# A fused attention and mixture-of-experts kernel: a new order of the attention's steps, a third transposed q/k buffer, and sums of x spread over expert 1

## The chip, the core and the metric

The kernel runs on one core of a Trainium2 chip. A core has a tensor engine for matmuls (PE, with its weight loads shown apart as PEld), a vector engine (DVE), a scalar engine (ACT), a general engine (POOL) and a queue engine (SP), each with its own queue of instructions that it works off in order. Matmuls write to eight banks of PSUM; everything else lies in SBUF. Transfers are issued from a queue (SP or POOL, here also ACT at the start) and run on 16 shared DMA engines. The metric is the device time of one execution in microseconds.

## The reference, cut to what matters

```python
# attention: batch 8, heads 8, seq 576, head_dim 64, 128 features
def phi(x):
    proj = np.einsum('bhsd,df->bhsf', x, w_phi)
    proj = proj - np.max(np.abs(proj), axis=-1, keepdims=True)
    return np.concatenate([np.exp(proj), np.exp(-proj)], axis=-1)
q_p, k_p = (phi(q), phi(k))
kv = np.einsum('bhsf,bhsd->bhfd', k_p, v)
z = np.sum(k_p, axis=2)
num = np.einsum('bhsf,bhfd->bhsd', q_p, kv)
den = np.einsum('bhsf,bhf->bhs', q_p, z)[..., None] + 1e-06
attn = num / den
# experts: N = 4608 tokens, D = 512, E = 8, F = 1024; x is attn, heads side by side
logits = x @ w_gate
P = np.exp(logits - logits.max())
for _ in range(8):
    P /= P.sum(1, keepdims=True) + 1e-09
    P /= P.sum(0, keepdims=True) + 1e-09
    P *= N / E
for e in range(E):
    h = np.maximum(x @ w1[e], 0.0)
    out += P[:, e:e + 1] * (h @ w2[e])
```

Every expert works on every token; P only weighs its result.

## The kernel before, in words

**A plan, then four fixed queues.** The program first writes down operations, each with its engine, an estimated duration, and the keys that it reads and writes (`Plan.op`). Then `Plan.schedule` plays them: again and again it takes the operation that can start earliest by the estimates, and among equals the one written down first. `Clock` stands for the tensor clock, `Links` for the two transfer lines (one for SP's and ACT's transfers, one for POOL's). What comes out is a fixed order of instructions for each engine; on the chip each engine follows it and waits where data isn't there. So the order in which steps are written down, and every estimate, change the order on all queues, while the instructions stay.

**Buffers.** A `Ring` is a fixed number of slots of one shape; an operation that needs a slot waits until the slot's last user is done. The ones that matter: `qk` (2, half a batch of k and q in bf16), `v_m` (2, half a batch of v), `qkT` (2, k and q transposed, 4 KB per partition each), `qk_r` and `v_r` (2 each, the last 64 tokens of up to three batches), `hT` (4), and later `S` (5) and `X` (3).

**Attention** goes by pairs of heads, 32 in all, four to a batch, 512 of 576 tokens each; the last 64 tokens of every batch are "rests". The steps are letters. `a` (pair_a) multiplies a pair's transposed k with w_phi (L568), takes maxima on DVE (L560), exponentials on ACT (L564), and v times a factor on POOL (L756). `q` does the q scores and their maxima, `p` the transposed q features. `b` (pair_b) makes the k-v products, `n` and `m` the two heads' outputs (L851, L859 to L865), `c` (pair_c) transposes them into xT, which is on the tensor engine for batches 0, 1, 2 and 7 and by a DMA from SP for 3, 4, 5 and 6 (L874). `r` and `g` are the rests' counterparts of `a` and `c`; `g` also makes the routing logits. `u` and `d` are quarters of a group's up and down products of expert 0, plain matmuls of 512 columns, 24 and 20 of which stand among the attention's steps.

k and q of batches 0 and 1 are loaded as fp32 into buffers that are still empty and transposed on the tensor engine (L698). Those of batches 2 to 7 are loaded by POOL in half batches and converted to bf16 on the way (L496), and turned by a DMA transpose on SP (`turn_qk`, L513, 512 KB). In the kernel before, a load and its turn are issued inside step `a` of the batch ahead: at pairs 0 and 2 of batch b the halves 0 and 1 of batch b+1, each after the maxima of q of the pair before (the key `("max", 0, i - 1)`). Expert 0's weights come in eight slices at pairs 2 to 9, from POOL: four of W1 by columns (L472), four of W2 by rows (L477). An up unit reads the W1 slice of its own columns.

**After the attention** its buffers are given back ("late"), the eight rounds of routing run on DVE with a small matmul each (L1104 to L1115), and what is left of expert 0 runs on the tensor engine. Experts 1 to 7 run over nine groups of 512 tokens with seven products in place of eight for a 2 by 2 blocking (`up7`, `down7`, all matmuls at L1250). That needs four differences of blocks of x per group, `sums_x` (L1158, S<-xT): they are written to DRAM (`xd`, L1234) and read back for every expert (L1240, X<-xd). Before, all nine groups' sums are written down ahead of expert 1, each in two slots of S; `down7` uses four slots of S per group for its own differences of hT.

The lines that carry the steps of the change:

```python
gt = [("max", 0, i - 1)] if i >= 1 else []        # stage_a: the load's gate
ring(a_t, [128, 2, 8, 128], BF16, "qkT", 2)
if e == 1:
    for g in range(NG):
        sums_x(g)
```

Of the kernel before, what the change touches and what calls it, by code (L numbers as in the profile page):

```python
# [108 lines left out]
class Op:  # L109
    __slots__ = ("eng", "dur", "lat", "nbytes", "fn", "left", "ready", "users", "idx", "end",  # L110
                 "bufs", "deps", "shared", "turn", "tiled")

    def after(self, user):

        if user.eng == self.eng and not self.nbytes:
            return self.end - self.lat + (0.0 if self.eng == "PE" else 0.04)
        return self.end


class Links:  # L120
# [6 lines left out]
    def add(self, o, at):  # L127
        n = int(o.eng == "POOL")
        self.line[n].append([at + (2.6 if n else 1.65), o.nbytes / 1e3, o])
# [4 lines left out]
    def step(self, t, work):  # L134
# [5 lines left out]
        if len(on) == 2:  # L140
            share = [0.23, 0.59] if self.line[0][0][2].turn else [0.59, 0.42]
# [48 lines left out]
class Plan:  # L190
# [9 lines left out]
    def op(self, eng, dur, lat, fn, r=(), w=(), takes=(), nbytes=0, shared=False):  # L200
# [5 lines left out]
        o.shared, o.turn, o.tiled = shared, False, 0  # L206
# [42 lines left out]
    def schedule(self):  # L249
# [22 lines left out]
        while len(done) < len(self.ops) or links.next():  # L272
# [28 lines left out]
            else:  # L301
                o.end = at + dur + o.lat
# [11 lines left out]
def kernel(  # L314
# [74 lines left out]
    SPEED = {320: 322, 150: 171, 230: 400, 250: 311, 280: 415, 90: 226, 148: 216, 160: 300}  # L389

    def dma(queue, nbytes, rate, fn, r=(), w=()):

        o = plan.op(queue, 0.8 if queue == "POOL" else 0.6, 0.0, fn, r, w, (),
                    nbytes / SPEED.get(rate, rate))
        o.turn = rate == 148
# [25 lines left out]
    ring(a_in, [128, 3 * NP, 2, D], BF16, "qk_r", 2)  # L421
    ring(a_in, [128, 3 * NP, D], FP32, "v_r", 2)
    ring(a_t, [128, NP, 128], BF16, "rT", 2)
    ring(a_t, [128, 2, 8, 128], BF16, "qkT", 2)
# [42 lines left out]
    def load_w0(i, r):  # L467
# [3 lines left out]
        if i < 4:  # L471
            dma("POOL", 1 << 19, 250, lambda: nc.gpsimd.dma_start(  # L472
                out=w1()[:, :, n * 256:(n + 1) * 256],
                in_=moe_w1[0].rearrange("(c p) f -> p c f", p=128)
                [:, :, n * 256:(n + 1) * 256]), r, [(w1, n)])
# [442 lines left out]
    def up(w1, g, hT, fcs, n, r=(), w=()):  # L918

        for f0 in fcs[::n]:  # L920
            ph = new(f"P{n}")
            ht = hT[f0 // 4]
            for i in range(n):
                for dc in range(NP):
# [3 lines left out]
                        xkeys(g, dc) + [(w1, (f0 + i) // 2), *r], [ph, *w], [ht])  # L928
# [80 lines left out]
    def stage_a(i):  # L1009
        b, pr = i // 4, i % 4  # L1010
        st[i], ms[i], qs[i] = pair_a(b, pr, halves[b, pr // 2])
        gt = [("max", 0, i - 1)] if i >= 1 else []
        if b + 1 < B and pr in (0, 2):
            if b + 1 > 1:
                halves[b + 1, pr // 2] = new_half(b + 1, pr // 2)
            t = halves[b + 1, pr // 2]
            load_qk(b + 1, 2 * pr, 4, t, gt)
            load_v(b + 1, 2 * pr, 4, t, gt)
            if b + 1 >= 2:
                turn_qk(t)  # L1020
        if pr == 1 and b in (0, 1, 4):
            load_rests(b + 1, 1 if b == 0 else 3, gt)
        n = i - 2
        if 0 <= n < 8:
# [483 lines left out]
```

The softmax here doesn't subtract the row's maximum and nothing guards it: scores larger than these inputs give would overflow.

## Time and profile before

| | us |
|---|---|
| median of 6 executions | 1040.15 (1037.38 to 1043.19) |
| the profiled execution's own time | 1041.22 |
| its span, first to last instruction | 1039.4 |
| PE busy, of the span | 1016.6 (98%) |
| PEld | 840.2 (81%) |
| DVE | 821.2 (79%) |
| ACT | 706.3 (68%) |
| POOL | 459.4 (44%) |
| mean granted tensor clock | 0.998 |

How to read it: a matmul's record lasts longer than its place in the pipeline (273 ns for 256 columns, where the next one starts 109 ns later), so a PE that is 98% busy may still lose time; the distance between starts tells. The chain that ended last is followed back from the end, at each step to what released it. A row of the windows has the stretch, its length, then busy time and number of instructions of PE, PEld, DVE, ACT and POOL, the granted clock, the mean busy share of the DMA engines (over 1 where transfers overlap on an engine) and GB/s. SPq is SP's queue; the number after the start is how long the issuing took. In the waits, the three numbers are us in total, times, and the longest.

Stages of the profiled execution: attention with parts of expert 0 to about 213 us, routing and the rest of expert 0 to 263.3, experts 1 to 7 to the end.

### The profile page before, as it was taken

The page shows a single profiled execution, that of the slowest core. Times are in us where ns is not written, and L with a number is a line of the kernel's source. Part 1 is how long each engine was busy: PE and PEld are TensorE (multiplying, and loading weights), DVE is VectorE, ACT ScalarE, POOL GpSimd, SP SyncE. Part 2 cuts the span into 40 slices and gives each one's busy share as a digit, 9 for nine tenths or more (in the row PEclk, how much of TensorE's full clock was granted, in tenths as well). Part 3 has the DMA queues.
Part 4 walks back from the last instruction along what each step waited for, and adds up shares of the span by engine and source line. Part 5 has one row for each costly group of instructions (what it writes and reads, how often), then busy time and mean ns, then how long its engine had stood idle before and what let it go on. Part 6 is the DMA issues. An engine that isn't in the chain of part 4 may idle for free.

```text
span 1039.4 us, 24345 instructions
## 1 busy us (share of the span) xinstructions
PE 1016.6 (98%) x9512; PEld 840.2 (81%) x9512; DVE 821.2 (79%) x1576; ACT 706.3 (68%) x1530; POOL 459.4 (44%) x476
## 2 busy tenths in 40 slices
PE   7889999999999999999999999999999999999998
PEld 5556666644888888888888888888888888888886
DVE  8979998788777787778777887788778877787775
ACT  7979999833788866566666665666666656666663
POOL 5867675400244444434443444344444443334442
PEclk9999999999999999999999999999999999999999
DMA  9999987274511161114311341134111611114333
GB/s 245 160 166 182 178 157 138 43 182 132 103 42 47 47 122 47 48 42 85 80 41 52 82 93 42 42 68 95 42 51 43 132 42 42 42 42 123 133 123 122
DMA packets 113939, 96.02 MB, mean 92 GB/s; under 512 B 54048, under 2 KB 88992, under 8 KB 113824
## 3 DMA queue, kind: packets, MB, share of 16 engines
q1 hardware_dynamic: 80544, 70.55, 27.1%
q0 software_dynamic: 33120, 23.86, 17.2%
q8 instruction: 74, 1.21, 0.5%
q14 instruction: 41, 0.34, 0.1%
q10 hardware_dynamic: 160, 0.07, 0.0%
HBM read 94.98 MB, written 14.16 MB: 105 GB/s over the span
## 4 chain that ended last, share of the span: by engine, by line
PE 89%; DMA 6%; ACT 2%; DVE 1%; POOL 1%; issue 1%; SPq 0%; DVEq 0%; POOLq 0%; ACTq 0%
PE ps L1250 74%; PE ps L568 14%; DMA qkT<-qk 4%; PE ps L851 1%; DMA xd<-S 1%; ACT k L564 0%; DMA acc<-in_q_dram 0%; DMA xT<-xb 0%; ACT q L564 0%; ACT kr L564 0%; POOL vrd L678 0%; PE ps L698 0%; SPq L546 0%; ACT qr L564 0%; POOL qk L496 0%
## 5 line engine op out<-in xcount | busy, mean ns | idle before, releaser
L1405 POOL TENSOR_TENSOR acc<-acc,V 128x512 f32<-128x512 f32 x248 | 316.3, 1285 | 435.3 <-ACT V L1402 418.0
L1278 ACT COPY U<-ps 128x512 f32<-128x512 f32 x378 | 217.3, 587 | 171.9 <-PE ps L1250 162.7
L1282 DVE CUSTOM_DVE_ANT_0 hT<-ps,U 128x512 bf16<-128x512 f32 x378 | 254.3, 686 | 82.8 <-PE ps L1250 57.9
L1402 ACT ACTIVATE V<-ps,P 128x256 f32<-128x256 f32 x496 | 208.7, 474 | 85.6 <-PE ps L1250 78.0
L1390 DVE SCALAR_TENSOR_TENSOR acc<-ps,P,acc 128x256 f32<-128x256 f32 x372 | 159.6, 477 | 78.9 <-PE ps L1250 78.7
L1250 PEld LDWEIGHTS <-S 128*128 128x128 bf16 x1984 | 194.1, 98 | 22.7 <-issue 0.2
L1250 PEld LDWEIGHTS <-T 128*128 128x128 bf16 x1512 | 147.9, 98 | 17.1
L1250 PEld LDWEIGHTS <-hT 128*128 128x128 bf16 x1488 | 145.6, 98 | 16.8
L1250 PE MATMUL ps<-X,T 128*128 128x256 bf16 x1008 | 151.2, 273 | 0.0
L1250 PE MATMUL ps<-T,S 128*128 128x256 bf16 x1056 | 135.8, 273 | 0.1
L1250 PEld LDWEIGHTS <-wx 128*128 128x128 bf16 x1152 | 112.7, 98 | 13.6 <-issue 0.2
L1158 DVE TENSOR_TENSOR S<-hT 128x1024 bf16<-128x1024 bf16 x124 | 87.7, 721 | 9.8 <-ACT hT L1287 9.8
L1250 PEld LDWEIGHTS <-w 128*128 128x128 bf16 x864 | 84.5, 98 | 9.8
L1250 PE MATMUL ps<-xT,wx 128*128 128x256 bf16 x576 | 88.7, 273 | 0.0
L1250 PE MATMUL ps<-X,wx 128*128 128x256 bf16 x576 | 86.5, 273 | 0.0
L1287 ACT ACTIVATE hT<-ps 128x512 bf16<-128x512 f32 x126 | 72.6, 606 | 7.7 <-PE ps L1250 7.7
L1250 PE MATMUL ps<-wx,hT 128*128 128x256 bf16 x560 | 77.6, 273 | 0.0
L1250 PE MATMUL ps<-xT,T 128*128 128x256 bf16 x504 | 76.4, 273 | 0.0
L568 PE MATMUL ps<-xT,w 128*128 128x512 bf16 x288 | 74.7, 379 | 0.0
L568 PE MATMUL ps<-w,hT 128*128 128x512 bf16 x288 | 73.0, 379 | 0.0
L1250 PE MATMUL ps<-T,hT 128*128 128x256 bf16 x496 | 68.4, 273 | 0.0
L1250 PE MATMUL ps<-xT,w 128*128 128x256 bf16 x432 | 67.3, 273 | 0.0
(127 smaller groups left out, 1420.1 us busy)
## 6 DMA issues: line engine op xcount, KB each, us to landing
X<-xd SPq DMA_DIRECT2D x126, 256.0 KB, 2.6
wx<-in_moe_w_dram POOLq DMA_DIRECT2D x8, 1024.0 KB, 10.2
v_m<-in_v_dram SPq DMA_DIRECT2D x15, 512.0 KB, 6.0
out_dram<-acc SPq DMA_DIRECT2D x14, 512.0 KB, 3.1
w<-in_moe_w_dram POOLq DMA_DIRECT2D x6, 1024.0 KB, 9.6
xd<-S SPq DMA_DIRECT2D x18, 256.0 KB, 4.5
qk<-in_k_dram POOLq DMA_DIRECT2D x12, 256.0 KB, 6.1
qk<-in_q_dram POOLq DMA_DIRECT2D x12, 256.0 KB, 7.1
```

The costliest lines, as they stand in the source:

```text
L568: nc.tensor.matmul(out_, lhsT=lhsT, rhs=rhs, start=start, stop=stop)
L851: pe(65, lambda j=j: nc.tensor.matmul(pn()[:, j * D1:j * D1 + D1], lhsT=s["T"][x]()[:, j % 2, 2 * h + j // 2, :] if j < 4 else r["T"][x]() ...
L1158: lambda: f.tensor_tensor(out=out_(), in0=x(), in1=y(), op=op), r, w, **kw)
L1250: pe(256, lambda i=i, k=k, z=z: nc.tensor.matmul(bank()[:, 256 * i:256 * i + 256], lhsT=lhs(k, i), rhs=rhs(k), start=first and z, stop=k = ...
L1278: act(512, lambda: nc.scalar.copy(out=u[fp][n]().rearrange("p a b -> p (a b)"), in_=x[fp]()), [x[fp]], [u[fp][n]])
L1282: dve(515, lambda: nc.vector._custom_dve(ADD_SAT, out=out_(fp, i, j), in0=bank[fp]().rearrange("p (a b) -> p a b", a=2), in1=u[fp][n](), s ...
L1287: act(512, lambda: nc.scalar.activation(out=out_(fp, i, j), in_=x[fp]().rearrange("p (a b) -> p a b", a=2), func=ACT.Relu, bias=0.0, scale ...
L1390: dve(320, lambda n=n, ts=ts: nc.vector.scalar_tensor_tensor(out=acc[g][:, ts, 256 * j:256 * j + 256], in0=bank()[:, 256 * n:256 * n + 256 ...
L1402: act(370, lambda n=n: nc.scalar.activation(out=u()[:, n, :], in_=bank()[:, 256 * n:256 * n + 256], func=ACT.Copy, bias=0.0, scale=P[:, 4 ...
L1405: pool(695, lambda: nc.gpsimd.tensor_tensor(out=acc[g][:, 2 * i:2 * i + 2, 256 * j:256 * j + 256], in0=acc[g][:, 2 * i:2 * i + 2, 256 * j: ...
```

## The change

- The ring `qkT` has 3 slots; `qk_r` and `v_r` hold two batches per slot, not three.
- Loads (`l`), turns (`t`), rests' loads (`e`) and weight slices (`w`) are letters of the order of their own. A load waits for the newest maxima of q and of k written down before it.
- The order is another string. Parts of it that the prediction speaks of: the first load of batch 2 stands behind pair 2, its second behind pair 4; the first two turns behind pairs 5 and 7; two W1 slices behind pair 2, one behind each of pairs 4 and 5; the four of W2 behind pair 8; the first `u` behind the `c` of pair 4. Rests are loaded for 1, 1, 2, 2 and 2 batches.
- W1 of expert 0 is cut by the contracted rows; an up unit needs all four slices.
- `sums_x` is written down for groups 0 and 1 ahead of expert 1, and for group g+2 between group g's up and down products of expert 1, after one of the blocks of hT.
- The planner's estimates change: end of an operation on its own engine, time to the first byte (1.45 and 2.5 us), rates of transfers, and shares of two lines in use together.

```diff
-        self.line[n].append([at + (2.6 if n else 1.65), o.nbytes / 1e3, o])
+        self.line[n].append([at + (2.5 if n else 1.45), o.nbytes / 1e3, o])
...
-            share = [0.23, 0.59] if self.line[0][0][2].turn else [0.59, 0.42]
+            a, b = (x[0][2] for x in self.line)
+            all_ = (0.6 if a.turn else 0.88) / (a.unit + b.unit)
+            share = [all_ * a.unit, all_ * b.unit]
...
-    SPEED = {320: 322, 150: 171, 230: 400, 250: 311, 280: 415, 90: 226, 148: 216, 160: 300}
+    LINK = {320: (312, 55), 150: (168, 28), 230: (410, 66), 250: (300, 50), 280: (410, 54),
+            270: (400, 90), 90: (270, 37), 148: (215, 23), 160: (470, 40)}
...
-    ring(a_in, [128, 3 * NP, 2, D], BF16, "qk_r", 2)
-    ring(a_in, [128, 3 * NP, D], FP32, "v_r", 2)
+    ring(a_in, [128, 2 * NP, 2, D], BF16, "qk_r", 2)
+    ring(a_in, [128, 2 * NP, D], FP32, "v_r", 2)
     ring(a_t, [128, NP, 128], BF16, "rT", 2)
-    ring(a_t, [128, 2, 8, 128], BF16, "qkT", 2)
+    ring(a_t, [128, 2, 8, 128], BF16, "qkT", 3)
...
-            dma("POOL", 1 << 19, 250, lambda: nc.gpsimd.dma_start(
-                out=w1()[:, :, n * 256:(n + 1) * 256],
-                in_=moe_w1[0].rearrange("(c p) f -> p c f", p=128)
-                [:, :, n * 256:(n + 1) * 256]), r, [(w1, n)])
+            dma("POOL", 1 << 19, 270, lambda: nc.gpsimd.dma_start(
+                out=w1()[:, n, :], in_=moe_w1[0].rearrange("(c p) f -> p c f", p=128)[:, n, :]),
+                r, [(w1, n)])
...
-                        xkeys(g, dc) + [(w1, (f0 + i) // 2), *r], [ph, *w], [ht])
+                        xkeys(g, dc) + [(w1, dc), *r], [ph, *w], [ht])
...
-        gt = [("max", 0, i - 1)] if i >= 1 else []
-        if b + 1 < B and pr in (0, 2):
-            if b + 1 > 1:
-                halves[b + 1, pr // 2] = new_half(b + 1, pr // 2)
-            t = halves[b + 1, pr // 2]
-            load_qk(b + 1, 2 * pr, 4, t, gt)
-            load_v(b + 1, 2 * pr, 4, t, gt)
-            if b + 1 >= 2:
-                turn_qk(t)
-        if pr == 1 and b in (0, 1, 4):
-            load_rests(b + 1, 1 if b == 0 else 3, gt)
-        n = i - 2
-        if 0 <= n < 8:
-            load_w0(n, gt)
+
+    def gates():
+
+        seen = order[:at[0]]
+        return [("max", x, seen.count(n) - 1) for x, n in ((0, "q"), (1, "a")) if n in seen]
+
+    def stage_l(n):
+        b, i = 1 + n // 2, n % 2
+        if b > 1:
+            halves[b, i] = new_half(b, i)
+        load_qk(b, 4 * i, 4, halves[b, i], gates())
+        load_v(b, 4 * i, 4, halves[b, i], gates())
+
+    def stage_e(n):
+        load_rests(*((1, 1), (2, 2), (4, 2), (6, 2))[n], gates())
...
-        "arqparqbabqbapqnbaqamqmbnpabqpnpbmnpccnrcnpamqcaqpmbupaqumcacrnbqnuanbqampun"
...
+        "lalareapqbwwlqanalqwaptrwaebbqpnmcpaqtpbmcpmnaqbqwwnmwncrmpcbmqqbwclutpnuapm"
...
     for i, n in enumerate(order):
+        at[0] = i
         STEPS[n](order[:i].count(n))
...
-    def sums_x(g):
+    def sums_x(g, r0=()):
...
-                xkeys(g) + ["late"] + [(X[i // 2], i % 2) for i in r]
+                xkeys(g) + ["late", *r0] + [(X[i // 2], i % 2) for i in r]
...
         if e == 1:
-            for g in range(NG):
+            for g in range(2):
                 sums_x(g)
...
             un = up7(A7, g, X, hT, ["up0"])
+            if e == 1 and g + 2 < NG:
+                later = (g + 2, [(hT[1], 0, 1)])
...
             if dn is not None:
                 dn["out"]()
+            if e == 1 and g + 2 < NG:
+                sums_x(*later)
```

## The prediction

> **What bounds the kernel now.** I read four views of the one profiled execution: the chain that ended last, the stages in windows, the tensor engine's timeline, the SP queue's timeline.
>
> The chain comes first, in order of time. Its second number is a length.
>
> ```profile
> 37.46 16.81 DMA qkT<-qk
> 54.31 1.96 PE ps L568 x9
> 56.27 16.54 DMA qkT<-qk
> ...
> 215.05 7.80 DMA xd<-S
> ...
> 263.34 158.07 PE ps L1250 x1445
> 421.45 606.58 PE ps L1250 x5555
> 1028.04 6.92 PE ps L568 x32
> ```
>
> From 263.34 on the chain is tensor work without a break: 7000 matmuls of 256 columns in 764.7 us, 109.2 ns each, and back to back this shape takes 109. So 776 us (263.3 to 1039.4) are fixed as long as the matmuls stay: the change removes none. What can move is the time at which expert 1 starts, 263.3. Ahead of it the chain names two places: the transposes by DMA (qkT) at 37 to 73, and the writes of the x sums (xd) at 215.
>
> Then the windows: PE busy, weight loads, DVE, ACT, POOL, granted clock, DMA share, GB/s.
>
> ```profile
> 30.00:40.00 10.00, 8.11 (x106) 5.21 (x105) 10.00 (x27) 10.00 (x25) 9.89 (x18) 1.00 1.61 199
> 40.00:50.00 10.00, 8.65 (x119) 6.27 (x120) 9.63 (x25) 9.18 (x23) 6.86 (x11) 1.00 1.45 97
> 50.00:60.00 10.00, 7.12 (x61) 4.22 (x58) 5.46 (x13) 6.44 (x16) 4.88 (x8) 0.83 1.39 179
> 60.00:70.00 10.00, 9.11 (x97) 5.17 (x95) 8.42 (x23) 8.89 (x24) 5.46 (x11) 1.00 1.51 129
> 70.00:80.00 10.00, 8.52 (x114) 5.72 (x112) 9.06 (x21) 9.24 (x25) 8.44 (x12) 1.00 1.26 184
> 80.00:90.00 10.00, 9.89 (x111) 6.72 (x108) 9.31 (x23) 9.29 (x23) 6.91 (x12) 1.00 1.07 187
> ...
> 220.00:230.00 10.00, 7.97 (x39) 3.55 (x38) 7.54 (x22) 3.07 (x6) 0.00 (x0) 1.00 1.13 272
> ```
>
> To 50 us ACT and DVE are nearly full; between 50 and 60 every engine falls back and the granted clock is 0.83: all wait for transfers.
>
> Busy PE overlaps itself, so I took the starts of the matmuls in the timeline and subtracted from each distance what the shape takes back to back (216 ns for 512 columns, 109 for 256, 56 for 128 and 130, 30 for 65, 110 for fp32, 28 for the gate's). The excess is lost time. To 263.3 us the matmuls are 228.8 us of work, the first starts at 3.7, and some 31 us are lost: by tens of us 3.9, 2.5, 2.7, 4.7 to 40; 2.4, 4.8, 2.1, 2.5 to 80; 0.55 and 0.51 to 100; 2.6 in all from 80 to 212; 2.4 at 222. No reordering can gain more.
>
> The timelines show what the row 50:60 waited for.
>
> ```profile
> 54.31 1.89 PE L568 MATMUL ps<-wphi,qkT 128*128 128x256 bf16 x8 [2.88 <-DMA qkT<-qk]
> ```
>
> ```profile
> 34.91 0.37 SPq L504 DMA_DIRECT2D v_m<-in_v_dram  x1
> 37.46 5.42 SPq L513 DMA_TRANSPOSE qkT<-qk  x1
> 42.99 0.51 SPq L504 DMA_DIRECT2D v_m<-in_v_dram  x1
> 43.69 9.95 SPq L632 DMA_TRANSPOSE rT<-qk_r  x2
> 56.27 8.11 SPq L513 DMA_TRANSPOSE qkT<-qk  x1
> ```
>
> What SP waited for, by line, first from 20 to 36 us and then from 44 to 58:
>
> ```profile
> SPq L504 <- POOL m L754: 10.0, 1, 10.0
> ```
>
> ```profile
> SPq L513 <- PE ps L568: 2.5, 1, 2.5
> ```
>
> Batch 2's first half is turned only at 37.46: the queue stood 10.0 us for a v slot (to 34.91) and then for q's landing (the POOL issue at 25.19 landed at 36.5). It lands at 54.3. The second half is issued at 56.27, when two rest turns have left the queue and, 2.5 us on, pair 7's matmuls have read the qkT slot that it needs; those stood at the tensor engine behind the wait for the first half. It lands at 72.8.
>
> **The change part by part.** It issues the same matmuls, exponentials and maxima; batches 3 to 6 turn x by DMA in the old kernel too.
>
> *A third qkT slot, turns and loads as steps of their own.* With two slots batch 2's halves need those of pairs 4 and 5, and of 6 and 7; with three, those of 2 and 3, and of 4 and 5. The old order read the last of pair 5's slot at 37.4 and makes a pair in some 7 us (11 v products by 80 us), so the second turn can go near 40 and not 56.3. The first is bound by its slot near 33 and by q's landing; for that l(2) stands behind pair 2 where the old load stood behind pair 4, l(3) behind pair 4 (before: 6). Each l moves two POOL issues (0.75 to 0.84 us) past pairs' POOL products (1.91 each) and a v load on SP; each t goes past v loads in SP's queue. A first turn issued at 33 that takes the old 16.8 us lands at 50, ahead of the 51.4 at which PE ran dry; the second lands by 57, 16 us earlier than before. Lost time from 40 to 80 is 11.8; the rows 80 to 100 show 0.53 per 10 us in the same mix, so 9.7 is the most. I take the row 50:60 less that floor (4.3) and half of the excess of the other three ((2.4+2.1+2.5-1.6)/2 = 2.7), since ACT and DVE at 9 of 10 limit them too: 7.0. The other end is a turn still late once and one more gap of 4.8: a loss of 4.8. I stay near the gain because 1.4 us earlier is enough for the first turn, and the second has 16.
>
> The Trainium skill (Advanced Engine Details and Errata, X-Bar Transpose) says transposing DMAs are as fast as plain ones, 350 to 400 GB/s. By that 512 KB would be an estimated 1.4 us, nearly all of the 16.8 would be standing behind other transfers, which a slot doesn't shorten, and this part would bring 2.7 and the sum 5.4. The rows speak against it: the fastest of the twelve turns took 4.3 us and the median 6.9, where 256 KB by a plain load (X<-xd) take 2.6.
>
> *Expert 0's weights.* W1 comes as four slices of the contracted rows (one run of 4 KB per partition) instead of columns (four runs of 1 KB). Slices took 8.5 to 12.3 us to land, W2's with 2 KB runs 14.2 to 18.2 in the busier stretch: the trace doesn't separate run length from load. I cost it at nothing. Against it, the first up unit now needs all four slices, not one. The fourth was issued at 35.15, so landed near 44.4; the first up matmul ran at 41.8. That would be 2.6 us late, but u0 stands behind c4, not b7, and pair work lies in front of it; without that cover it costs 2.6. A gain is excluded: the old first unit's slice was issued at 20.29 and landed by 32.6 at the slowest.
>
> The skill's rule (DMA: Bandwidth & Descriptors, Specifications) that 512 B is enough for line rate would also make the slices worth nothing.
>
> *Gates and rests.* A load now waits for the newest key and query maxima placed before it. Behind a gated POOL issue stand that queue's products v times em (1.91 us), and behind those the kv matmuls. The old trace has such a case: POOL idle 4.1 us ahead of the qk issue at 54.80. From 80 to 130 POOL is idle 1 to 5 of 10 us, so I take nothing; bounds 0 and 4.1. The rests come as 1, 1, 2, 2, 2 batches, not 1, 1, 3, 3: four more POOL issues (4 x 0.8 = 3.2 us) and two more on SP (1.3 us), under the same idle time.
>
> *The first 40 us.* Batch 0's rest (r0) moves behind pair 1's keys. The old order loses 0.8 and 0.6 us around its transposes (9.7 to 11.4); I take 1.0. The rest is ACT and DVE at 9.3 to 10: bounds +2 and -2.
>
> *80 to 212.* 2.6 us are lost in all; take 0, between a gain of 1.5 and a loss of 3.7 (the one wait on xT by DMA in the chain).
>
> *x sums.* Before, 36 subtractions of 0.41 us stand among the routing's steps on DVE; SP writes 18 tiles, five slots S hold them, and at 222.88 DVE stands 2.18 us for a slot while the routing's matmul waits: the 2.2 us of the row 220:230. With two groups ahead four slots are enough, so the 2.2 go; expert 0's matmuls cover the rest as now. The other 28 subtractions go into expert 1, four per group and ahead of down7's. Starts are 0.33 to 0.41 us apart, so 1.3 to 1.6 us per 12.2 us group, where DVE is busy 8.98 and idle 1.51 + 0.30 + 0.92 + 0.29 + 0.18. The group at 373.1 runs with DVE at 11.15 and an unbroken chain, so I take 0.5 for all seven. The bound is slots: the sums hold two of five while the write flies (4.5 us in the old trace, 2.6 for the loads back); if down7's subtraction waits 2.18 as at 222.88, less the 1.51 idle, 0.67 x 7 = 4.7.
>
> Sum: 7.0 + 0 + 0 + 1.0 + 0 + 2.2 - 0.5 = 9.7. The profiled execution's own time is 1041.2 (span 1039.4 and 1.8 around it), so 1031.5; it stands 1.1 above the median 1040.15, which makes 1030.5.
>
> **The rivals.**
> A. *The transfers are the bound and the gap only moves.* For it: from 20 to 75 us the DMA share is 1.2 to 1.6 and landings take 8 to 18 us, so an earlier issue may just queue longer. Against: W2's slices now stand behind pair 8, out of the turns' way, and the row 50:60 has engines idle, not only DMA. Gain 0 to 3 (r0, xd): 1037 to 1041, middle 1039.
> B. *Slower: a turn at the head of SP's queue holds what pairs need.* A t that waits there for its slot or its qk blocks the v loads and the turns of rests and x behind it, and it runs beside more of POOL's loads, which is how it came to 16.8 us. The old queue shows a wait of 10.0 at its head. Place: 40 to 110 us. Price: one late turn costs PE 4.8 (row 50:60). If the old gap stays (7.0 of the sum gone: 1037.5), one new late turn makes 1042.3, no change; from two on it is slower: 1047.1. Against: with three slots each turn has half a batch more to land in.
> C. *Slots S in expert 1:* -4.7 instead of -0.5: 1030.5 + 4.2 = 1034.7.
>
> **How the numbers follow.** The forecast's own case (1024 to 1033) gets 0.60, C 0.08, A 0.12, B 0.20. 0.3%, about what a measurement of this kernel can tell from no change, is 3.1 us, 1037.0 to 1043.3. Faster is the forecast and C, 0.68; the same is A, 0.12; slower B, 0.20. The low end takes the best of each part (9.7 for 40 to 80, 2 for the start, 1.5 for 80 to 212, 2.4 for the x sums: 15.6 from 1040.15, 1024.6, and 1 us for the spread between runs): 1023.5. The high end takes in A and the near half of B, up to one late turn and a half: 1044.5.
>
> **What would show it.** Right: the first qkT turn issued before 34 us and landed before pair 8's matmuls; granted clock 1.00 from 50 to 60; qkT's share of the chain from 4.5% to under 2.5%; no DVE wait for xd<-S in the routing; the first L1250 matmul near 253.5, and from there to the end 776 to 777. Wrong: a new tensor wait on qkT, xT or w beyond 2 us before 110; a tail of 779 or more, with DVE's S<-hT waiting for xd; or POOL idle before gated issues with kv matmuls behind.

## The result and the profile after

The changed kernel takes 1042.87 us (median of 31 runs, 1040.17 to 1047.71) against 1040.26 for the kernel before (68 runs, 1033.8 to 1045.01): a ratio of 1.0032, 95% interval 1.0019 to 1.0044. The interval leaves out 1, so the kernel is slower, by 2.6 us. The forecast was 1030.5, which is faster, and 1042.87 lies inside its range, 1023.5 to 1044.5. The profiled execution took 1045.0 us (span 1043.3, clock 0.996). That is 3.8 us more than the one before, 1.2 more than the medians differ by, so 1.2 of the two traces' difference is the draw of these two executions.

The queue of SP, first. Columns are start, length of the issue, line and tiles.

```profile
32.72 2.02 SPq L518 DMA_TRANSPOSE qkT<-qk  x1
...
42.79 3.04 SPq L518 DMA_TRANSPOSE qkT<-qk  x1
...
57.22 11.28 SPq L509 DMA_DIRECT2D v_m<-in_v_dram  x2
69.51 10.45 SPq L518 DMA_TRANSPOSE qkT<-qk  x2
...
115.05 3.04 SPq L518 DMA_TRANSPOSE qkT<-qk  x1
```

Batch 2's halves are turned as forecast: issued at 32.72 and 42.79 (before: 37.46 and 56.27) and landed at 37.1 and 49.2 (before: 54.3 and 72.8). The first took 4.4 us and not 16.8. But batch 3's first half is turned only at 69.51 (the row there joins both of its halves), and batch 4's second half at 115.05. The chain that ended last (start, length) shows what followed, and where the late x sums come in:

```profile
53.61 4.25 DMA rT<-qk_r
...
69.51 10.97 DMA qkT<-qk
80.52 7.33 PE ps L573 x26
...
115.05 7.26 DMA qkT<-qk
...
268.54 7.22 DMA xd<-S
275.85 1.27 DVE S L1168
```

The tensor engine's timeline has the two waits in attention:

```profile
80.52 2.74 PE L573 MATMUL ps<-wphi,qkT 128*128 128x256 bf16 x12 [3.69 <-DMA qkT<-qk]
...
122.36 1.05 PE L573 MATMUL ps<-wphi,qkT 128*128 128x256 bf16 x8 [2.35 <-DMA qkT<-qk]
```

The windows of after (the last three columns are the granted clock, the DMA share and GB/s):

```profile
50.00:60.00 10.00, 8.94 (x109) 5.98 (x107) 9.45 (x22) 9.94 (x26) 7.83 (x12) 1.00 0.97 117
...
70.00:80.00 10.00, 6.81 (x100) 4.55 (x96) 6.84 (x19) 7.74 (x22) 3.43 (x5) 0.97 1.21 152
80.00:90.00 10.00, 9.48 (x71) 5.50 (x72) 6.34 (x11) 6.52 (x16) 7.92 (x13) 0.68 0.79 150
...
120.00:130.00 10.00, 7.65 (x92) 5.30 (x92) 7.25 (x17) 6.68 (x18) 7.77 (x12) 1.00 0.99 144
...
270.00:280.00 10.00, 7.75 (x68) 6.44 (x67) 7.62 (x13) 7.13 (x15) 4.13 (x3) 1.00 0.58 148
```

The hole of 50:60 is gone, and two new ones stand at 70:90 and 120:130. Behind the wait that ended at 80.52 the clock granted in 80:90 was 0.68. A third hole is in expert 1. Two rows of the kernel before for the same stretches:

```profile
120.00:130.00 10.00, 10.00 (x120) 6.41 (x117) 9.40 (x22) 10.00 (x28) 5.26 (x11) 1.00 1.52 183
...
270.00:280.00 10.00, 10.00 (x92) 8.73 (x91) 7.71 (x13) 9.57 (x20) 2.60 (x3) 1.00 0.43 113
```

With the prediction's own measure (starts of matmuls, less what the shape takes back to back), lost time in us by stretch:

| stretch | before | after | change | forecast |
|---|---|---|---|---|
| 0 to 40 | 13.8 | 13.7 | -0.1 | -1.0 |
| 40 to 80 | 11.8 | 8.9 | -2.9 | -7.0 |
| 80 to 210 | 2.6 | 6.7 | +4.1 | 0 |
| 210 to 260 (routing) | 2.6 | 2.1 | -0.6 | -2.2 |
| 260 to 280 (expert 1, first group) | 0.3 | 2.9 | +2.5 | } +0.5 |
| 280 to the end | 1.4 | 2.2 | +0.8 | } |
| sum | 32.6 | 36.4 | +3.8 | -9.7 |

The sum of the changes, 3.8, is the difference of the two executions' times.

A second measure proved steadier than the sum: the first seven-product matmul of expert 1, and the time from there to the end. Before: 263.2 and 776.2. After: 263.6 and 779.7.

### The profile page after: what moved, and what is told of

Same layout as the page of the kernel before. It is cut to its first block, busy times and chain, and to the rows that moved or that the text cites. A ratio compares the mean times of both kernels' runs of the same rounds, so it can differ in the third digit from the quotient of the medians.

```text
span 1043.3 us, 24320 instructions
## 1 busy us (share of the span) xinstructions
PE 1017.3 (98%) x9512; PEld 839.0 (80%) x9512; DVE 827.1 (79%) x1576; ACT 706.0 (68%) x1530; POOL 461.5 (44%) x480
## 4 chain that ended last, share of the span: by engine, by line
PE 86%; DMA 5%; DVE 5%; ACT 2%; issue 2%; POOL 1%; SPq 0%; POOLq 0%; DVEq 0%; ACTq 0%
PE ps L1260 70%; PE ps L573 14%; DMA qkT<-qk 2%; PE ps L856 1%; DMA wx<-in_moe_w_dram 1%; DVE m L565 1%; DMA xd<-S 1%; ACT k L569 1%; DMA acc<-in_q_dram 1%; DMA rT<-qk_r 0%; ACT q L569 0%; DVE hT L1292 0%; DVE cs L1120 0%; DMA qk_r<-in_q_dram 0%; DVE wx L565 0%
## 5 line engine op out<-in xcount | busy, mean ns | idle before, releaser
L1260 PEld LDWEIGHTS <-S 128*128 128x128 bf16 x1984 | 194.1, 98 | 24.5 <-issue 2.0
L1260 PEld LDWEIGHTS <-T 128*128 128x128 bf16 x1512 | 147.9, 98 | 17.2
L1260 PEld LDWEIGHTS <-hT 128*128 128x128 bf16 x1488 | 145.6, 98 | 17.8 <-DVE hT L1292 0.5
L1260 PE MATMUL ps<-X,T 128*128 128x256 bf16 x1008 | 150.7, 273 | 0.0
L1260 PE MATMUL ps<-T,S 128*128 128x256 bf16 x1056 | 135.7, 273 | 0.6 <-DVE acc L1400 0.5
L1260 PEld LDWEIGHTS <-wx 128*128 128x128 bf16 x1152 | 112.7, 98 | 13.3
L1260 PEld LDWEIGHTS <-w 128*128 128x128 bf16 x864 | 84.5, 98 | 10.6 <-issue 0.7
L1260 PE MATMUL ps<-xT,wx 128*128 128x256 bf16 x576 | 89.2, 273 | 0.0
L1260 PE MATMUL ps<-X,wx 128*128 128x256 bf16 x576 | 86.7, 273 | 0.9 <-DVE hT L1292 0.9
L1260 PE MATMUL ps<-wx,hT 128*128 128x256 bf16 x560 | 77.0, 273 | 0.8 <-DVE hT L1292 0.8
L1260 PE MATMUL ps<-xT,T 128*128 128x256 bf16 x504 | 76.1, 273 | 0.0
L1260 PE MATMUL ps<-T,hT 128*128 128x256 bf16 x496 | 68.7, 273 | 0.0
L1260 PE MATMUL ps<-xT,w 128*128 128x256 bf16 x432 | 67.3, 273 | 0.0
```

Source lines behind the costliest of these rows:

```text
L1260: pe(256, lambda i=i, k=k, z=z: nc.tensor.matmul(bank()[:, 256 * i:256 * i + 256], lhsT=lhs(k, i), rhs=rhs(k), start=first and z, stop=k = ...
```

## What held batch 3's turn

Late is meant against the tensor engine, not against the kernel before. Two rows of SP's queue there are the turns of the same halves, batch 3's first and batch 4's second:

```profile
71.57 4.50 SPq L513 DMA_TRANSPOSE qkT<-qk  x1
...
102.79 5.04 SPq L513 DMA_TRANSPOSE qkT<-qk  x1
```

Batch 3's first half landed at 80.38 before and at 80.48 after, in these two traces. It came no earlier, while the tensor engine, without the old gap, was ready for it at 76.8, and it stood there until 80.5. Before, it waited less than 0.5 us for that turn. Batch 4's second half did come later: landed at 114.71 before, at 122.3 after.

POOL's timeline of after shows what the turn at 69.51 stood behind:

```profile
59.33 0.76 POOL L482 DMA_DIRECT2D w<-in_moe_w_dram  x1
...
60.30 0.78 POOL L482 DMA_DIRECT2D w<-in_moe_w_dram  x1
...
63.50 0.83 POOL L501 DMA_DIRECT2D qk<-in_k_dram  x1
64.33 0.76 POOL L501 DMA_DIRECT2D qk<-in_q_dram  x1
```

and the list of SP's waits from 44 to 72 us:

```profile
SPq L509 <- POOL v L767: 10.5, 1, 10.5
```

Batch 3's k and q are issued behind the four slices of expert 0's W2 (55.56 to 60.30), and q landed at 69.36. In the same while SP's queue stood 10.5 us at its head for a v slot and went on at 68.1. So both queues let the turn go only near 69. It then ran beside the second half's k, q and v and took 10.97 us. Batch 4's second turn (115.05) went 0.6 us after its q had landed (114.49). Its loads went out at 105.58 and 108.45, where the kernel before issued them at 89.73 and 90.57: in POOL's new queue they stand behind the loads of two batches' rests and a step that waited 4.07 us for DVE's maxima.

## The experiments

Each kernel is compared with the kernel before on the same chip. "Start" and "tail" are the first seven-product matmul of expert 1 (L1250 before, L1260 after) in the profiled execution, and the time from there to the end. In the variants that move steps, the finished list of each engine's queue is edited: `(what, its queue, ahead of what, on which queue)`.

### The late turn, moved up

```diff
+MOVES = [("l4", "POOL", "w4", "POOL"),   # batch 3's load ahead of W2's slices
+         ("t2", "SP", "l4", "SP")]       # its turn ahead of its v load
```

> The changed kernel with two moves in the finished instruction order and nothing else: batch 3's first loads of k and q go ahead of W2's four slices on POOL, and its turn goes ahead of the v load of the same half on SP. Theory (the gap was moved: a turn that is issued late because its loads stand behind W2's slices and its place in the SP queue behind a v load that waits for a slot to 68.1 us): k and q are issued near 56 us and not 63.5, the turn is issued by 64 and not 69.5 and lands by 70 and not 80.5; the tensor engine's wait of 3.9 us at 76.5 and the slow clock behind it (0.68 in 80 to 90) go; time lost from 70 to 90 falls from 7.0 to under 2.5, the time by 4 to 6 us against the changed kernel, to 1037 to 1039 or a ratio of 0.996 to 0.999 to the kernel before. Rival (transfers as a whole, or the lack of other tensor work, are the bound): the turn lands earlier, but a new gap of 3 us or more opens between 76 and 130 (W2's slices or v are late now) and the time stays within 1 us of the changed kernel's 1043.

1042.5 us, ratio 1.0025 (1.0002 to 1.0047). The wait at 76 is gone, and in its place stand two others:

```profile
61.04 1.03 PE L582 MATMUL ps<-wphi,rT 128*128 128x256 bf16 x4 [3.89 <-DMA rT<-qk_r]
...
74.76 0.59 PE L582 MATMUL ps<-w,hT 128*128 128x512 bf16 x2 [2.62 <-DMA w<-in_moe_w_dram]
```

The turn itself went at 62.96 and took 12.3 us. The time is what the rival said: in this order a rest's turn and W2 are late in its place. A second place for the load, ahead of the third W1 slice:

```diff
+MOVES = [("l4", "POOL", "w2", "POOL"), ("t2", "SP", "l4", "SP")]
```

> The changed kernel with the same turn made early in another place: batch 3's first loads of k and q go ahead of the third W1 slice on POOL (some 37 us, where the DMA share was 0.66 to 1.1), and the turn ahead of the v load on SP as in the run before. In that run the gap at 76 went and two others came, at 57 for a rest's turn and at 72 for W2's slices, since loads and turn ran beside both. Theory (a turn needs a stretch in which POOL's loads don't run beside it; there is room at 37 to 45): the turn is issued by 59 and lands by 67, the rest's turn keeps its 4 to 5 us, no tensor wait above 1.5 us between 50 and 100, lost time 50 to 100 falls from 9.9 to 5 or less, the time by 3 to 6 us against the changed kernel. Rival (the transfers of 20 to 130 us are the bound as a whole): another transfer is late instead, a wait of 2.5 us or more somewhere between 45 and 130 that neither kernel had, time within 1.5 us of the changed kernel.

1046.92, ratio 1.0067 (1.0042 to 1.0091): worse. The tensor engine's waits from 40 to 90, and one window:

```profile
PE ps L582 <- DMA w<-in_moe_w_dram: 4.9, 3, 2.1
```

```profile
70.00:80.00 10.00, 6.98 (x53) 3.82 (x53) 3.46 (x7) 4.37 (x10) 4.51 (x9) 0.66 1.04 153
```

Now both of expert 0's weights are late, 4.9 us in three waits, and the clock of 70:80 is 0.66.

### Take the weights away

If the transfers of this stretch are the bound, leaving W2's 2 MB out must mend it. Three kernels do so, on the moved order, on the changed one and on the one before: the four loads keep their place in the plan but issue nothing, and one POOL instruction zeroes W2's tile at the start. Expert 0's part is missing from their output.

> The order of the first of these runs with an early turn (batch 3's loads ahead of W2's slices, its turn ahead of the v load) with W2's four slices of expert 0 left out: the tile is set to zero once at the start, so expert 0's part is missing from the output; every other instruction keeps its place. Theory (the transfers between 20 and 130 us are the bound, so that with W2 in the way a gap can only be moved): with 2 MB read less the third turn takes 4 to 7 us and not 12.3, the rest's turn keeps to 5, no tensor wait above 1.5 us from 50 to 100; lost time 50 to 100 falls from 11.4 to 5 or less, the time by 4 us or more against the same order with W2. Rival (the order of the queues, not the amount of transfers): another late transfer takes its place, lost time 50 to 100 stays at 9 or more.

> The changed kernel with W2's slices of expert 0 left out in the same way (tile set to zero, expert 0's part missing from the output), no move. Theory (transfers are the bound): POOL comes to batch 3's loads 2 to 3 us earlier and nothing runs beside its turn but them; the turn still stands behind the v load that waits for its slot to about 68, so it's issued at 67 to 69 and lands by 75: the wait at 76 shrinks from 3.9 to under 1.5 us, time 2 to 5 us under the changed kernel. Rival (the turn is late by its place in the SP queue alone): turn and gap stay as they are, the time within 1 us of the changed kernel.

> The kernel before with W2's slices of expert 0 left out in the same way. Theory (the first turn took 16.8 us because W2's slices and the next half's loads ran beside it, not because a slot was missing): the first turn is still issued at 37 to 38, lands by 46 and the gap at 51 to 54 is gone (lost time 50 to 60 from 4.8 to under 2), though qkT has two slots; the time falls by 4 us or more, to 1034 to 1037. Rival (the slot is what made it late): the second turn is still issued after 52 and a tensor wait on qkT of 2 us or more stays between 48 and 75.

With the turn early and W2 away: 1039.76, ratio 0.9999 (0.9978 to 1.0019), 2.7 us less than with W2 (the theory had 4 or more). Its SP queue and one window:

```profile
63.38 1.32 SPq L534 DMA_TRANSPOSE qkT<-qk  x1
```

```profile
70.00:80.00 10.00, 9.98 (x122) 6.85 (x121) 9.72 (x25) 10.00 (x29) 5.86 (x11) 1.00 0.72 135
```

The same turn, 0.4 us later in issue, lands after 4.26 us and not 12.34, and no wait over 1.5 us is left between 50 and 100. So W2's slices made that turn long. On the changed order W2 is not the whole of it: 1041.6, ratio 1.0024 (1.0003 to 1.0046), with a wait of 2.0 us left, which ends at 79.55. There the turn stays late by its place (70.73) and lands 8.8 us on, beside the next half's loads. On the kernel before it gave 1037.04 (0.9967, 0.9945 to 0.9989), but batch 2's first turn still took 36.50 to 52.4. So it isn't W2 that makes that one long; the theory fell, though the time, 0.33% down, came near its range. Beside that turn ran the fourth W1 slice, batch 2's own second half and, from 42 us, a v load and a rest's turn; none of them was taken away, so which of them it was isn't shown.

### The third slot, alone and taken away

```diff
-    ring(a_t, [128, 2, 8, 128], BF16, "qkT", 3)
+    ring(a_t, [128, 2, 8, 128], BF16, "qkT", 2)
```

> The changed kernel with two qkT slots and not three; the planner orders anew. Theory (the third slot is what let the first two turns go at 32.7 and 42.8): the first turn is issued at 37 or later, the second at 50 or later, a tensor wait on qkT between 45 and 65 of 3 us comes back: 1046 to 1049. Rival (the turns are quick, 4.4 us and not 16.8, because loads no longer crowd them; the slot isn't needed): no wait over 1.5 us between 40 and 65, time within 1.5 us of the changed kernel.

1048.42, ratio 1.0084 (1.0056 to 1.0111), 5.5 us above the changed kernel. Its two turns:

```profile
36.28 4.62 SPq L518 DMA_TRANSPOSE qkT<-qk  x1
52.07 3.04 SPq L518 DMA_TRANSPOSE qkT<-qk  x1
```

Back near the times of the kernel before, 37.46 and 56.27. So the slot does set when these turns go, but where the 5.5 us went isn't shown: the tensor wait of 3 us on qkT that was expected from 45 to 65 isn't in the trace, and the trace is of the fastest of six executions, 1045.14. The reverse, three slots in the old order (`qkT` 3, rests two batches at a time to make the room):

> The kernel before with a third qkT slot; to make room, the rests of batches 2 to 7 are loaded by twos (at pair 1 of batch 1, pair 2 of batches 3 and 5), so qk_r and v_r are as in the changed kernel. Order string, planner's estimates, weight slices and sums are the old ones. Theory (the slot alone brings part of the 7 us that the prediction gave to 40 to 80): first turns issued by 36 and by 47, the gap of 4.8 in 50 to 60 halves, 1036 to 1039. Rival (crowding: the old order issues W1, W2, rests and halves together, so that turns take 12 us or more whatever the slot): the first turn still lands after 48, the gap stays, 1039 to 1042.

```profile
35.82 5.00 SPq L513 DMA_TRANSPOSE qkT<-qk  x1
...
47.84 7.20 SPq L513 DMA_TRANSPOSE qkT<-qk  x1
```

1047.57, ratio 1.0079 (1.0049 to 1.0109): slower than theory and rival had it, though the second turn went 8.4 us earlier. The two took 11.2 and 13.3 us to land, but the old gap isn't in this trace: from 10 to 78 us no tensor wait is over 1 us, and none of those that show is for a transfer. What it lost came later, with a wait of 2.28 us for a rest's turn at 106.75, one of 2.15 on qkT at 164.99, and half the clock three times for 3.41 us; this trace is of the slowest of eight executions, 1051.72. So the slot is worth some 5.5 us in an order that was made for it. In the old order the gap went, and more was lost behind it; the changed rests are part of this kernel too, and the run doesn't part them from the slot.

### The clock after the gap

Twenty filler matmuls of 256 columns were put into the kernel before, ahead of the matmuls that wait at 54.31, to keep the clock up:

```diff
+for _ in range(20):
+    nc.tensor.matmul(bank()[:, 0:256], lhsT=wphi2[:, 0, :], rhs=wphi2f, start=True, stop=True)
```

> The kernel before with 20 matmuls of 256 columns (2.2 us of tensor time, their result is overwritten) put ahead of the matmuls that wait for batch 2's first turn at 51.4 to 54.3. Theory (half of what a late turn costs is the clock that is granted after it, and whether it is lowered differs from execution to execution): the granted clock stays at 1.00 from 50 to 62, the slow executions at 1041 to 1044 disappear and the median falls to 1035 to 1037, the time that the kernel before has at a mean clock of 1.000. Rival (the spread is something else, and the gap costs what it lasts): the median stays within 1 us of the kernel before, or rises by up to 2.2.

1039.57, ratio 1.0007 (0.9985 to 1.0029). The half clock at 54 is gone from its profile, but another stands at 224.7 (6.83 us) beside a wait in the routing. A fall of 3 us or more, as the theory promised, lies outside the interval; the time is what the rival said.

### The x sums

All nine groups of sums ahead of expert 1, as before:

```diff
-            for g in range(2):
+            for g in range(NG):
                 sums_x(g)
-            if e == 1 and g + 2 < NG:
-                sums_x(*later)
```

> The changed kernel with all nine groups' sums of x written down ahead of expert 1 again, as in the kernel before; the attention's part is the same. Theory (the sums in expert 1 cost 2.5 us, once, because the first group's writes of S run beside the load of an expert's weights and come back after 7 us): the DVE wait of 2.35 us at 273.5 goes, time lost from 260 to 300 falls from 2.9 to under 0.5, and the routing's wait comes back (time lost from 220 to 260 up from 2.0 to 2.5 or more): 1040.5 to 1043. Rival (spreading the sums is worth the 2.2 us that the prediction gave it): the time goes up by 1 to 2 us, to 1044 to 1045.

1037.97, ratio 0.9986 (0.9964 to 1.0007): faster than either account had it. The wait at 273.5 went, as the theory said, but the routing's wait, which should have come back, didn't. Only the first group of expert 1 left free of sums, three groups ahead:

```diff
-            for g in range(2):
+            for g in range(3):
-            if e == 1 and g + 2 < NG:
+            if e == 1 and g and g + 2 < NG:
```

> The changed kernel with three groups' sums ahead of expert 1 and none in its first group, where an expert's weights are loaded. Theory (the wait at 273.5 is a write of S that runs beside that load, 7.2 us where later writes take 2.0 to 3.9): no DVE wait for xd<-S after 263, lost time 260 to 300 under 0.6 (2.9 before), time 2 to 3 us under the changed kernel, 1040 to 1041. Rival (five slots are too few for both in any group): the wait comes back one group later, at some 285 us, and the time stays at 1042 to 1044.

1040.63, ratio 1.0001 (0.9979 to 1.0023), as the theory had it. The DVE timeline of the changed kernel shows what the first group pays:

```profile
275.85 1.27 DVE L1168 TENSOR_TENSOR S<-hT,S 128x1024 bf16<-128x1024 bf16 x1 [2.35 <-DMA xd<-S]
```

DVE stands 2.35 us for a slot of S; down7's sums for the first group stand behind it, and the tensor engine behind them. The write that holds the slot was issued at 268.54 and landed 7.2 us later, at 275.76, while the load of expert 2's weights (264.01 to 275.58) was under way. The median write of the 18 takes 2.1 us. No run took that load away, but the kernel before shows the same within one trace: while expert 1's weights were loading (213.44 to 233.79), nine of its writes were issued up to 229.93 and took 5.5 to 8.9 us; the six from 238.08 on, with no weights loading and fewer writes at once, took 2.0 to 2.4.

The same two edits on the kernel before, sums spread over expert 1, and spread but not in its first group:

> The kernel before with only the sums of x moved as in the change. Theory (the spread sums cost some 4 us and bring nothing: the routing's rounds lose their cover and expert 1's first group waits for S): the wait of 2.2 us at 222.5 goes, but small waits of 0.2 us on cs come in each round, and 2.5 to 3 us are lost at 270 to 280: time 2 to 5 us up, 1042 to 1045. Rival (what the sums cost in the changed kernel depends on its own attention's end): time within 1 us of the kernel before, or below it.

> The kernel before with the sums of x spread over expert 1, three groups ahead and none in the first group. Theory (spread sums cost only where a write of S runs beside an expert's weights; without that they are worth the 2.2 us that the routing loses in the kernel before): 1 to 3 us under the kernel before, 1037 to 1039.5, no DVE wait on xd<-S after 262. Rival (routing rounds without sums between them lose as much in small waits on cs): within 1 us of the kernel before.

1039.01 (0.9976, 0.9952 to 1.0000) and 1041.93 (1.0024, 1.0002 to 1.0046). There the spread isn't a loss, though the same wait shows:

```profile
274.25 0.69 DVE L1158 TENSOR_TENSOR S<-hT,S 128x1024 bf16<-128x1024 bf16 x1 [1.15 <-DMA xd<-S]
```

half as long. The two medians stand in the reverse of what their tails say (777.3 and 776.4), so what the spread is worth in the old kernel stays open within 2 to 3 us either way.

### Once more, side by side

The changed kernel again, with the sums ahead again, and with W1 in column slices again, all on one chip:

> The changed kernel itself once more, on the chip of the three runs beside it, as their control. All accounts: 1041 to 1044, a ratio of 1.001 to 1.005; where its own gaps are fixed by the order, lost time of 2 us or more at 270 to 280 and a tensor wait on qkT at 76 and near 119 come back in this profile; where they are chance, they are elsewhere.

> The changed kernel with all sums of x ahead of expert 1, again, now beside its control. Theory (the spread sums cost the changed kernel 3 to 5 us: the wait for S in expert 1's first group and the routing's rounds without cover): 3 to 5 us under the control, 1037 to 1040. Rival (the 5 us of the first run were a matter of chip and executions): within 1.5 us of the control.

```diff
-                out=w1()[:, n, :], in_=...[:, n, :]), r, [(w1, n)])
+                out=w1()[:, :, n * 256:(n + 1) * 256],
+                in_=...[:, :, n * 256:(n + 1) * 256]), r, [(w1, n)])
```

> The changed kernel with W1's slices of expert 0 cut by columns as before (runs of 1 KB read and 512 B written, not 4 KB and 2 KB), in the changed kernel's order, so that only the shape of four transfers differs. Theory (long runs leave the other transfers more room; the slices land in 5.8 to 8.2 us now, 8.5 to 12.3 before): the last two slices take 8 us or more, the second turn (42.8) lands 1 to 4 us later, lost time 40 to 70 rises by 1 to 3 us, time 0 to 3 us above the control. Rival (the slices landed faster because fewer loads ran beside them, the run length is worth nothing, as the prediction had it): same landings within 1 us, time within 1 us of the control.

1042.61 (1.0037, 1.0016 to 1.0057), 1040.6 (0.9998, 0.9978 to 1.0018) and 1044.47 (1.0045, 1.0022 to 1.0069). The changed kernel's holes came back in its second trace, smaller: waits on qkT of 2.28 us at 80.18 and 1.59 at 119.11, and one of 1.94 for S. The first of them is in all five traces with this order of the attention and these loads (2.28 to 3.69 us), so it belongs to the order and not to one execution. The sums ahead are worth 2.0 us here, less than the theory's 3 to 5, and 4.9 in the first run. Column slices cost 1.9 us, and the two intervals overlap: not told from nothing. Their shape doesn't show in the landings: the four took 6.3 to 8.7 us in columns and 6.5 to 8.4 in the control.

The tails, which no attention step touches, part the kernels better than the medians:

| kernels | tail, us |
|---|---|
| kernel before, with its variants that leave the sums alone (four) | 776.0 to 776.3 |
| changed kernel, with its variants that keep the spread (eight) | 778.9 to 779.7 |
| changed kernel, sums ahead (three, with the one below) | 776.6 to 777.4 |
| changed kernel, first group left free | 776.8 |

So the spread costs the changed kernel some 2.2 us in every profiled execution, and all of it in the first group, since the kernel that spares only that group has it back. The start of expert 1 tells the other half. The kernel before and its two variants with other sums start it at 258.0, 262.0 and 263.2; the changed one, in two executions, and its three variants with other sums at 260.4 to 263.6. The attention and routing came out even within that scatter. The medians differ by 2.6 us, and the tails, 779.0 against 776.2 in the mean, by 2.9.

### A version that beats both

Sums ahead; batch 3's load behind two of W2's slices and ahead of the other two; its turn ahead of its v load; and a later load (l7) ahead of the rests e2.

```diff
+MOVES = [("l4", "POOL", "w6", "POOL"), ("t2", "SP", "l4", "SP"), ("l7", "POOL", "e2", "POOL")]
```

> The changed kernel with all sums ahead and three moves: batch 3's first loads between W2's second and third slice on POOL, its turn ahead of the v load on SP, and the loads of batch 4's second half ahead of the rests' loads on POOL (so that its turn isn't late at 119). Theory (two late turns are left once the sums are back, and half of W2 out of the way is enough for the first): both waits on qkT fall under 1.5 us, 2 to 5 us under the run with the sums ahead alone, 1033 to 1036. Rival (transfers are the bound from 50 to 130, the gap moves): a wait on a rest's turn, W2 or v of 2 us or more takes their place, within 1.5 us of the run with the sums ahead.

1037.02 us, ratio 0.9968 (0.9948 to 0.9989): 3.0 us faster than the kernel before, 5.6 faster than the changed one on the same chip, 3.6 faster than with the sums ahead alone. By the ratios it is 1.9 us faster than the first run with the sums ahead, on another chip, and the intervals overlap. POOL's timeline, then the windows:

```profile
59.41 0.81 POOL L510 DMA_DIRECT2D qk<-in_k_dram  x1 [0.24 <-issue]
60.22 0.75 POOL L510 DMA_DIRECT2D qk<-in_q_dram  x1
60.95 0.72 POOL L491 DMA_DIRECT2D w<-in_moe_w_dram  x1
```

```profile
70.00:80.00 10.00, 9.93 (x136) 7.15 (x136) 9.56 (x24) 9.53 (x26) 5.30 (x12) 1.00 1.13 147
80.00:90.00 10.00, 9.88 (x131) 6.68 (x131) 9.83 (x22) 9.86 (x25) 8.43 (x15) 1.00 1.07 196
...
120.00:130.00 10.00, 9.85 (x127) 6.42 (x127) 9.29 (x24) 9.03 (x22) 9.10 (x15) 1.00 1.41 180
```

The load goes 4.1 us earlier than in the changed kernel and the turn 3.0 (66.51), two slices of W2 go after it, and W2 costs the tensor engine 0.5 us: both holes are closed, no clock drop, and the longest wait from 40 to 130 is 1.4 us. The hole behind batch 4's turn closed with it; the run has three moves and doesn't part them. The time misses the theory's 1033 to 1036 by 1 us; the rival, that the transfers are the bound from 50 to 130 us and the gap can only move, falls with this run.

## Why the prediction was wrong, step by step

**The 776 us after 263.3, fixed.** The matmuls are, the stretch isn't: it grew to 779.7, which was one of my signs of being wrong. That is the x sums, below.

**The third slot, 7.0.** For batch 2's turns the mechanism was right and its signs came: first turn before 34 us, clock 1.00 from 50 to 60, qkT's share of the chain from 4.5% to 1.7%, no wait on it before 76. From 40 to 70 lost time fell by some 4.5 us. But a sign of being wrong came as well, a new tensor wait on qkT beyond 2 us before 110: 3.69. The step that failed is the end of the term, together with the 0 for 80 to 212: I followed batch 2's two turns, took it that the rest up to 80 would come down towards the 0.53 of the rows behind it, and never asked whether the turns behind came earlier too. Batch 3's first didn't: its load was behind W2, its turn behind a v load, it landed at 80.5 as before, and the gap came back there. Batch 4's second came 7.6 us later, and there a new one opened: 40 to 80 brought 2.9 and 80 to 210, priced at 0 with a worst case of 3.7, lost 4.1. Rival A, that the transfers are the bound and the gap moves, had 0.12, and its reason against ("W2's slices now stand behind pair 8, out of the turns' way") was wrong: behind pair 8 is in batch 3's way. The two early-turn kernels, the one without W2 and the last one show this by cause. A itself holds for this order only, since the last kernel closes the gap with the same transfers. B had the mechanism at SP's head (10.5 us for a v slot) and a price of 4.8 for each late turn, but with the old gap still there; what came was the old gap gone and two late turns, 6.0 us of waits together.

**What a turn takes.** I held the rows against the Trainium skill (Advanced Engine Details and Errata, X-Bar Transpose), by whose rate nearly all of 16.8 us would be standing behind others. The runs agree with that half of it: the turn that took 12.34 took 4.26 with W2 gone, and batch 2's went from 16.8 to 4.4. Taking "the old 16.8 us" for the new first turn was too long by 12 us. The 1.4 us that I had estimated from the page's rate, though, no run came near: the shortest of the turns in all traces took 4.24 us, which for 512 KB is 124 GB/s from issue to landing.

**W1's slices, 0.** Between 0 and a gain of 1.9; not told apart, and the landings are alike. The Trainium skill's 512 B for line rate (DMA: Bandwidth & Descriptors, Specifications), by which the price would be 0 too, is neither refuted nor shown.

**Gates and rests, 0.** My text said that a load "waits for the newest maxima". The keys order the plan; on the chip the issues stand where the queue has them (POOL's row at 63.50 shows no wait). Nothing that stands behind a load was seen to be late, but the price that was missed is the load's own place in the queue: batch 4's second half went out behind a wait of 4.07 us there.

**The first 40 us, -1.0.** Measured -0.1. A size off.

**The x sums, -1.7 in all.** Two sizes off, on both sides. The slot wait of 2.2 in the routing is gone, but the changed kernel with all sums ahead has no such wait either (0.8 to 0.9 us for `cs` is its longest), so the spread had nothing to gain there; it lost small waits of 0.2 on `cs` instead. In expert 1 the 0.5 was for seven groups by DVE's spare time. The bound that I named, slots, decides, but once and not seven times: 2.5 us in the first group, where the write runs beside the weights' load. I priced the write at 4.5 us, the median; the chain's own row of before, 215.05 with 7.80, was a write beside such a load. Rival C had 0.67 times 7; the wait is 2.35 times one.

**The sum.** The forecast was 13.5 us off in the traces: 4.1 + 4.1 for the moved gap, 0.9 for the start, 1.6 for the routing, 2.8 for expert 1. The chances 0.68, 0.12 and 0.20 gave most to a case that took each part at its first place only. By my own band, 1037.0 to 1043.3, what came is "the same", to which I had given 0.12; that it lies in the range at all is because the range took in rival A and half of B.

## What to carry to other kernels

Where transfers crowd for a hundred microseconds, a turn that goes earlier is worth only what the transfers behind it can spare: follow the next two loads of the same kind through each queue, and what else the queues put ahead of them, before the gain is counted. A place among other loads is worth more than the earliest one: behind two of four weight slices the load was late for nobody, ahead of all or behind all a wait of 2.3 to 3.9 us stood somewhere. Work that is spread into a later stage is priced at that stage's worst group, and the time from a stage's first instruction to the end shows 2 us when executions that scatter by 10 hide it.

## What was not expected of the hardware

**One transfer, four to seventeen us.** The 512 KB transpose took 4.2 to 4.4 us at best, 8 to 12.5 beside other half-batch loads or weight slices, 17.2 in the worst case. A write of 256 KB took 2.1 in the median (after) and 7.2 beside the next expert's weight load.

**The same queues, ten us apart.** The kernel before ran from 1033.8 to 1045.0 with the same instructions. From 40 to 80 us the kernel before lost 11.8 us in its profiled execution; its variant with the sums spread but not in the first group, with the same order up to there, lost 5.5, and batch 2's first turn took 9.8 us there and not 16.8. So the gap that the forecast was built on isn't in every execution.

**The clock falls for fixed lengths.** Around tensor waits the granted clock is half for 3.41 or 6.83 us: from 10 to 1030 us the traces have 17 such stretches, and none of another length. It was 3.41 at a wait of 2.9 (before, at 54), 6.83 at one of 3.7 (after, at 80), 6.83 at 3.2 and 3.41 at 3.0 in others, and it didn't fall at 2.35 (after, at 122). While it is half, matmuls of 256 columns start 213 ns apart and not 109, so such a wait costs up to another 1.7 or 3.4 us of tensor work. It doesn't go by the length of one wait: with the load moved ahead of the third W1 slice, 3.41 us of half clock began at 42.0, at a wait of 1.15, and with the turn early the clock stayed whole at 2.62. Nor do the stretches between lie anywhere: the full clock before lasts from 9.52 to 53.89, 13 times 3.413 us, and after from 7.81 to 79.49, 21 times. So where a wait falls against these windows may matter as much as how long it is; no run here tests it. The Trainium skill (TensorE: Matmul & The Clock Gate, Part 1) says that the clock falls after an idle window of about 3.4 us, that the window runs free, and that the number of slow matmuls differs between runs. The lengths agree with whole windows; that the engine must be idle through a whole one does not, by the wait of 1.15 and that of 2.9.
